# Attention with two head mixes and two MoE layers on one core: the second mix moved to a step's end, score and v pairs spread one a step, loads and early weights reordered

## The chip, the cores and the metric

One core of a Trainium2 chip runs the whole program. The metric is device time in microseconds (us) of one execution; the time of a kernel is the median of its runs. Engines are named as in the profile: PE is TensorE (matmuls), PEld its weight loads, DVE is VectorE, ACT is ScalarE, POOL is GpSimd, SP is SyncE, whose queue issues nearly all DMAs.

## What is computed

Attention over 2 batches, 12 heads, 448 rows and a head size of 64, with the scores mixed across heads before the softmax and the probabilities mixed across heads after it; then two feed-forward layers on the 896 x 768 result. The weights of these layers come as float64.

```python
scores = scale * np.matmul(q, k.transpose(0, 1, 3, 2))
scores = np.einsum('bhij,hg->bgij', scores, w_pre)      # first mix
scores = scores - np.max(scores, axis=-1, keepdims=True)
attn = np.exp(scores)
attn = attn / (np.sum(attn, axis=-1, keepdims=True) + 1e-09)
attn = np.einsum('bhij,hg->bgij', attn, w_post)         # second mix
out = np.matmul(attn, v)
...
h = x @ w_in                                            # 768 -> 2048
g = np.where(h > 0.0, h, np.exp(np.minimum(h, 0.0)) - 1.0)   # layer 1; layer 2: g = h * sigmoid(h)
x = g @ w_out                                           # 2048 -> 768
```

## The kernel before, in words

All order is written by hand: each engine runs its instructions in the order in which the program issues them.

**Attention in steps.** The 448 rows of a batch are cut into four tiles of 120, 120, 120 and 88 rows, eight tiles T = 0 to 7 in all. A tile's scores (12 heads x 448) are made by six "score pairs" (`qk_pair(T, p)`, L159: two heads each), scaled and copied to an SBUF tile `s` by ACT (head e = 0) and DVE (head e = 1) in `qk_evac` (L177). The mixes work on blocks of 10 rows x 12 heads; two blocks make a step. There are NB = 46 steps; the last step of each batch (22 and 45) has one block. The tiles begin at steps 0, 6, 12, 18, 23, 29, 35 and 41. For step s, `relayout(s)` (L196) brings two blocks of `s` by DMA on SP's queue into one of three buffers `blk`; it is issued two steps ahead. Then:

- `premix(s)` (L211): the first mix on PE into the two PSUM tiles `pre`; both are used by every step.
- `rmax(s)` (L218) on DVE: the negative maximum `nmx`; `exps(s)` (L224) on ACT: exponentials `pe` and their sums; `recip(s)` (L234): sum + 1e-9 and reciprocal on DVE, then two small scalings `krn` of the second mix's matrix on POOL (L243).
- `postmix(s)` (L246): the second mix on PE, 64 small matmuls on `pe` and `krn`, issued one step later, into one PSUM tile `post` of two banks; `post_evac` (L262) copies half of both banks to the tile `a` on ACT (L121), then the other half on DVE (L123).
- `av_pair(T, p)` (L274): the product with v for two heads of a finished tile.

One step of the loop issues, in this order: `premix(s)`, `postmix(s-1)`, the step's score pairs, v pairs and transposes (PE); `rmax(s)`, `exps(s)`, both halves of `post_evac(s-1)`, `qk_evac`, `recip(s)`, the v and transpose copies, `relayout(s+2)`, the step's loads. Tables `QK_AT`, `X_AT`, `KT_AT`, `D_AT` and `M_AT` say which step gets which pair, transpose, load or piece of weight work. Score pairs of tile T + 1 begin two steps ahead of tile T, and v pairs of tile T one step after tile T + 1 has begun, with what doesn't fit put into the last step; so step 21 has two score pairs and steps 23 and 46 two v pairs.

**Loads.** At the start q of tile 0, all of k of batch 0 (half of its DMAs issued from ACT's queue), the mix matrices; q has one buffer, so q of tile 1 is loaded when tile 0 is transposed. After the first two relayouts come v of batch 0 in two DMAs of 672 KB, then q of tile 2, which is transposed in steps 1 and 2.

**MoE.** Weights come as 64-bit words in chunks, 63 of them; a chunk is scaled on ACT (L480), turned into bits on DVE (L492, L494), and split into a high part (ACT, L508) and a low part (DVE, L514). A product is 18 matmuls (`moe_in`, L549): high x high, high x low, low x high over six slices. The first three chunks ("early", NE = 3) are loaded from step 39 on into the place of `s`, and one of their six products (chunk 1, first half of the rows) runs in thirds in the last steps. The input of the second half of the rows, `x1`, is split after the last step (`x1_hi`, `x1_lo`, L418).

## Time and profile before

| | us |
|---|---|
| runs | 728.5, 725.24, 725.59 |
| median | 725.59 |
| the profiled execution, its own time | 727.41 |
| its span, first to last instruction | 725.7 |
| PE busy in the span | 676.4 (93%) |
| DVE, ACT, POOL busy | 381.6, 343.7, 57.7 |

The span has two parts. From about 254 us to the end PE works through the MoE products without a pause. Before that lies the attention, where PE waits now and then. How the rows below are read: a row of the timeline gives start, length, engine, line, operation, out<-in and in brackets how long the engine sat idle before it and what ended that; a row of the waits gives who waited for whom, us in total, times, and the longest; a row of the chain is a piece of the path that ended last.

### The profile page before, as it was taken

How to read it: one execution, taken by the hardware profiler on the slowest of the kernel's cores; microseconds unless marked ns; L12 is line 12 of the kernel's file. 1: busy time of each engine (PE TensorE's matmuls, PEld its weight loads, DVE VectorE, ACT ScalarE, POOL GpSimd, SP SyncE). 2: the span in 40 equal slices, each digit the busy share in tenths (PEclk: the TensorE clock that was granted, in tenths of full speed). 3: DMA queues.
4: the chain of work that ended last, by engine and by line, in shares of the span. 5: the costliest groups of instructions: out<-in, count | busy, mean ns of one | idle time of the engine just before them, and what ended most of it. 6: DMA issues, size and time to landing. Idle time of an engine off the chain costs nothing.

```text
span 725.7 us, 16439 instructions
## 1 busy us (share of the span) xinstructions
PE 676.4 (93%) x6902; PEld 560.2 (77%) x6902; DVE 381.6 (53%) x771; ACT 343.7 (47%) x708; POOL 57.7 (8%) x118
## 2 busy tenths in 40 slices
PE   7667898788887899999999999999999999999998
PEld 3234555444554799999999999999999999999997
DVE  3535555555656556666664343336666667324500
ACT  2445666465675567666663233335555555313301
POOL 4011111122242100000000000000000000000000
PEclk8989999999999999999999999999999999999999
DMA  7545447424235133333353333333424345424202
GB/s 117 131 115 169 112 145 175 121 66 147 98 124 167 59 118 97 100 109 109 91 151 105 95 96 93 99 121 109 127 92 124 94 122 164 151 66 154 98 0 77
DMA packets 81866, 81.77 MB, mean 113 GB/s; under 512 B 25552, under 2 KB 77696, under 8 KB 81792
## 3 DMA queue, kind: packets, MB, share of 16 engines
q1 hardware_dynamic: 79008, 80.03, 37.0%
q10 hardware_dynamic: 2784, 0.69, 0.7%
q8 instruction: 54, 0.88, 0.5%
q14 instruction: 20, 0.16, 0.1%
HBM read 58.60 MB, written 2.75 MB: 85 GB/s over the span
## 4 chain that ended last, share of the span: by engine, by line
PE 78%; DVE 6%; ACT 6%; DMA 5%; issue 2%; POOL 2%; SPq 1%; ACTq 0%; POOLq 0%; DVEq 0%
PE ph L571 30%; PE po L624 16%; PE py L646 5%; PE py L644 5%; PE py L645 5%; ACT pe L230 3%; PE pre L216 3%; PE av L283 3%; PE pq L174 3%; PE post L256 3%; DMA blk<-s 3%; DVE a L123 2%; DVE s L183 2%; DMA qr<-in_q_dram 2%; DVE nmx L222 2%
## 5 line engine op out<-in xcount | busy, mean ns | idle before, releaser
L571 PE MATMUL ph<-x,we 128*128 128x448 f32 x1080 | 221.4, 367 | 0.0
L571 PEld LDWEIGHTS ph<-x,we 128*128 128x128 f32 x1080 | 202.8, 188 | 18.1
L624 PE MATMUL po<-g,we 128*128 128x448 f32 x468 | 101.3, 366 | 0.0
L256 PEld LDWEIGHTS post<-krn,pe 60*56 60x56 f32 (+1 forms) x2880 | 49.6, 134 | 59.7 <-POOL krn L243 57.5
L624 PEld LDWEIGHTS po<-g,we 128*128 128x128 f32 x468 | 87.9, 188 | 7.6
L230 ACT ACTIVATE pe<-pre,nmx 124x448 f32<-124x448 f32 (+1 forms) x92 | 57.5, 629 | 66.2 <-DVE nmx L222 54.6
L480 ACT ACTIVATE wr<-wr 128x384 f32<-128x384 f32 x126 | 67.3, 545 | 28.8 <-DMA wr<-in_moe_w_out_dram 24.9
L514 DVE TENSOR_TENSOR we<-wc,we 128x768 fp32r<-128x768 f32 (+1 forms) x63 | 58.7, 932 | 42.3 <-ACT we L508 39.4
L256 PE MATMUL post<-krn,pe 60*56 60x60 f32 (+1 forms) x2880 | 55.9, 222 | 26.6 <-POOL krn L243 26.2
L494 DVE SCALAR_TENSOR_TENSOR wc<-wr,wc 128x384 int32<-128x384 int32 x126 | 68.6, 545 | 5.3
L508 ACT CAST we<-wc 128x768 fp32r<-128x768 f32 (+1 forms) x63 | 50.8, 807 | 39.5 <-PE py L646 29.5
L123 DVE COPY a<-post 120x480 f32<-120x480 f32 (+1 forms) x46 | 30.9, 673 | 68.5 <-ACT a L121 68.5
L222 DVE TENSOR_REDUCE nmx<-pre 124x1 f32<-124x448 f32 (+1 forms) x92 | 53.0, 617 | 26.5 <-PE pre L216 25.9
L645 PE MATMUL py<-we,g 128*128 128x384 f32 x182 | 61.5, 338 | 0.0
L646 PE MATMUL py<-we,g 128*128 128x384 f32 x182 | 61.5, 338 | 0.0
L644 PE MATMUL py<-we,g 128*128 128x384 f32 x182 | 61.5, 338 | 0.0
L283 PEld LDWEIGHTS av<-a,v 120*64 120x64 f32 x768 | 37.6, 138 | 25.0 <-issue 17.3
L216 PE MATMUL pre<-blk,kpre 64*64 64x448 f32 (+1 forms) x360 | 51.2, 571 | 5.6 <-DMA blk<-s 4.6
L243 POOL TENSOR_SCALAR krn<-kps,sum 124x60 f32<-124x60 f32 (+1 forms) x92 | 41.1, 461 | 182.3 <-DVE sum L239 175.6
L174 PE MATMUL pq<-kt,qt 64*64 64x448 f32 (+2 forms) x384 | 50.1, 563 | 3.0 <-DVE s L183 2.3
L283 PE MATMUL av<-a,v 120*64 120x120 f32 (+1 forms) x768 | 46.8, 267 | 1.3 <-issue 1.3
L492 DVE TENSOR_SCALAR wc<-wr 128x384 int32<-128x384 int32 x126 | 43.7, 347 | 0.0
(86 smaller groups left out, 679.6 us busy)
## 6 DMA issues: line engine op xcount, KB each, us to landing
wr<-in_moe_w_in_dram SPq DMA_DIRECT2D x58, 384.0 KB
wr<-in_moe_w_out_dram SPq DMA_DIRECT2D x56, 384.0 KB
blk<-s SPq DMA_DIRECT2D x90, 210.0 KB
wr<-in_moe_w_out_dram SPq DMA_DIRECT2D x12, 256.0 KB
v<-in_v_dram SPq DMA_DIRECT2D x4, 672.0 KB
out_dram<-y SPq DMA_DIRECT2D x14, 192.0 KB
early<-in_moe_w_in_dram SPq DMA_DIRECT2D x6, 384.0 KB
qr<-in_q_dram SPq DMA_DIRECT2D x6, 360.0 KB
```

Source lines behind the costliest of these rows:

```text
L174: nc.tensor.matmul(pq[e][HS * c:HS * c + n], qT[T][half, p, HS * c:HS * c + n], kT[b, p][half], start=True, stop=True, tile_position=(e * ...
L216: nc.tensor.matmul(pre[s][r][HS * c:HS * c + HS], kpre[o], blkb[o, s % NBUF, c], start=True, stop=True, tile_position=(HS * r, HS * c))
L222: nc.vector.tensor_reduce(nmx[s][:n, r:r + 1], pre[s][r][:n], axis=AX.X, op=ALU.max, negate=True)
L230: nc.scalar.activation(t[:n], pre[s][r][:n], AF.Exp, bias=nmx[s][:n, r:r + 1], scale=1.0, accum_out=sums[s][:n, r:r + 1])
L256: nc.tensor.matmul(w[HS * u:HS * u + n, c, r * 240 + j * BW:r * 240 + (j + 1) * BW], pexp[s][r][o, j0:j0 + n], kr[s][r][o].rearrange("p h ...
L283: nc.tensor.matmul(avt[T][e * D:(e + 1) * D, p % 3, :m], vall[b][:NV, h, j], amap[T][:NV, j * H + h, :m], start=j == 0, stop=j == 3, tile_ ...
L494: nc.vector.scalar_tensor_tensor(cc, r[:, :, 1], 3, cc, op0=ALU.logical_shift_left, op1=ALU.bitwise_or)
L571: nc.tensor.matmul(ph, wt[:, kk * P:(kk + 1) * P], xq[hf, kk][:, xi], start=(n_ == 0), stop=(n_ + 1 == len(terms)))
L624: nc.tensor.matmul(po, wt[:, kk * P:(kk + 1) * P], g_out1(k0 + kk, gi, hf), start=(k0 == 0 and n_ == 0), stop=(k0 + kn == KF and n_ == 3 * ...
L644: nc.tensor.matmul(py, gh, hi[:, w_], start=(kf == 0), stop=False)
L645: nc.tensor.matmul(py, gh, lo[:, w_], start=False, stop=False)
L646: nc.tensor.matmul(py, gl, hi[:, w_], start=False, stop=(kf == KF - 1))
```

## The change

- A step now issues `premix(s)`, the score pair, the v pair, the transposes, any early MoE product, and `postmix(s-1)` as PE's last work; `post_evac(s-1)` is the last work of the step on ACT and DVE, behind the early weight work.
- `post` is two tiles of one bank, one for each block; ACT copies the first block and DVE the second. The score pair's two banks are separate tiles, too.
- One score pair and one v pair a step: score pairs run on without a gap (steps 0 to 39), v pairs from step 7 to 42, and those of tile 6 two a step in steps 43 to 45.
- q has two buffers; q of tile 1 is loaded right after the mix matrices, q of tile 2 right after the first two relayouts; v is loaded in four DMAs of 336 KB in steps 1 to 4 (batch 0) and 23 to 26 (batch 1).
- An exponential of one element on ACT stands ahead of ACT's loads; the clearing of `blk` goes from DVE to POOL.
- Early weights are loaded and turned in halves in steps 28 to 43, into the buffers of q and k. `x1` lies where `s` of the even tiles was, and its first 240 columns are split in steps 39 to 44 on ACT and POOL. Two of the early products (chunks 0 and 1, first half) run in thirds in steps 41 to 46.

```diff
-    cm_b, bp = pool("attn1", bufs=1, side="right")
+    cm_s0, sp0 = pool("s0", bufs=1, side="right")
+    cm_s1, sp1 = pool("s1", bufs=1, side="right")
...
-        r = raws["q", T] = bp.tile([TI, H, D], F32, name=f"qr{T}", tag="qr", bufs=1)
+        r = raws["q", T] = ap_.tile([P, H, D], F32, name=f"qr{T}", tag="qr", bufs=2)[:TI]
...
-        w = pst[s] = ps.tile([P, 2, 512], F32, name=f"post{s}", tag="post", bufs=1)
+        w = pst[s] = [ps.tile([P, 2, 4 * BW], F32, name=f"post{s}_{c}", tag=f"post{c}", bufs=1) for c in range(steps[s][2])]
...
-    def post_evac(s, r):
+    def post_evac(s):
...
-        o = amap[T][:NV, :, n * BI:(n + nc_) * BI].rearrange("p x (c r i) -> p c r x i", r=2, i=5)[:, :, r]
-        evac((nc.scalar, nc.vector)[r], o, pst[s][:NV, :nc_, r * 240:r * 240 + 240].rearrange("p c (x i) -> p c x i", i=5))
+        for c, w in enumerate(pst.pop(s)):
+            o = amap[T][:NV, :, (n + c) * BI:(n + c + 1) * BI].rearrange("p x (r i) -> p r x i", r=2)
+            evac((nc.scalar, nc.vector)[c], o, w[:NV].rearrange("p r (x i) -> p r x i", i=5))
...
+    wz = cp.tile([P, S], F16, name="wz")
+    nc.vector.memset(wz, 0.0)
+    nc.scalar.activation(kpre[0:1, 0:1], wz[0:1, 0:1], AF.Exp)
     load_q(0)
...
     load_mix()
+    load_q(1)
+    nc.gpsimd.memset(blkb[0:4], 0.0)
...
     for s in range(2):
         relayout(s)
-    for u in range(2):
-        load_v(0, u)
+    load_q(2)
...
-    load_q(2)
...
-                at(QK_AT, f - 2 + p, lambda T=T, p=p: qk_pair(T + 1, p))
...
+            if nqk >= 0:
+                at(QK_AT, nqk, lambda T=T, p=p: qk_pair(T + 1, p))
+            nqk += 1
...
+        for g in range(2):
+            at(D_AT, 1 + 2 * g + u, lambda u=u, g=g: load_v(0, u, g))
+            at(D_AT, first[4] + 2 * g + u, lambda u=u, g=g: load_v(1, u, g))
...
     def step(s):
         if s < NB:
             premix(s)
-        if 0 <= s - 1 < NB:
-            postmix(s - 1)
         run(QK_AT, s)
         run(X_AT, s)
         run(KT_AT, s)
+        run(F_AT, s)
+        if 0 <= s - 1 < NB:
+            postmix(s - 1)
         if s < NB:
             rmax(s)
             exps(s)
-        if 0 <= s - 1 < NB:
-            post_evac(s - 1, 0)
-            post_evac(s - 1, 1)
         qk_evac(0)
         qk_evac(1)
...
         relayout(s + 2)
         run(D_AT, s)
+        run(M_AT, s)
+        if 0 <= s - 1 < NB:
+            post_evac(s - 1)
...
+    for i, L in enumerate((-7, -4, -3, 0, 1, 4)):
+        n, j = divmod(i, 2)
+        at(M_AT, s6 + L + 2, lambda n=n, j=j: scale_w(n, j))
+        at(M_AT, s6 + L + 3, lambda n=n, j=j: bits_w(n, j))
+        at(M_AT, s6 + L + 3, lambda n=n, j=j: split_hi(n, j))
+        at(M_AT, s6 + L + 4, lambda n=n, j=j: split_lo(n, j))
+    for i, L in enumerate((-7, -4, -3, 0, 1, 4)):
+        at(M_AT, s6 + L, lambda i=i: load_w(i // 2, i % 2))
+    for n in range(2):
+        for part in range(3):
+            at(F_AT, NB - 5 + 3 * n + part, lambda n=n, part=part: moe_in(n, 0, n, 0, part))
```

PE's order around step 8, before: the end of the second mix of step 7, the step's score pair `pq`, v pair `av` and transpose `ptq`, and the first mix `pre` of step 9. The second mix of step 8 follows right behind it.

```order
L256 MATMUL post_795<-krn_1_784,pe_1_773 64x60 x2
L256 MATMUL post_795<-krn_1_784,pe_1_773 56x60 x2
L174 MATMUL pq_4_828<-kt_4_206,qt_356 64x448 x2
L174 MATMUL pq_4_828<-kt_4_206,qt_356 56x448 x2
L283 MATMUL av_0_752<-a_365,v_80 64x120 x8
L143 MATMUL ptq_1_841<-ident,qr_512 128x90 x3
L216 MATMUL pre_0_869<-blk,kpre 64x448
L216 MATMUL pre_1_870<-blk,kpre 64x448
```

The same step now: the first mix of step 8 (`pre_0_816`, `pre_1_817`), the same pairs and transpose, and only then the second mix of step 7.

```order
L214 MATMUL pre_0_816<-blk,kpre 64x448
L214 MATMUL pre_1_817<-blk,kpre 64x448
L172 MATMUL pq_4_0_822<-kt_4_212,qt_333 64x448
L172 MATMUL pq_4_1_823<-kt_4_212,qt_333 64x448
L172 MATMUL pq_4_0_822<-kt_4_212,qt_333 56x448
L172 MATMUL pq_4_1_823<-kt_4_212,qt_333 56x448
L280 MATMUL av_0_745<-a_388,v_83 64x120 x8
L145 MATMUL ptq_1_836<-ident,qr_527 128x90 x3
L254 MATMUL post_0_840<-krn_0_806,pe_0_798 64x60
L254 MATMUL post_1_841<-krn_0_806,pe_0_798 64x60
```

Between a step's first mix and its second mix on PE there stood one step's pairs; now there are two steps' pairs.

DVE's order in step 8, before: maximum, copy `a` of the second mix, copy `s` of the scores, then the two operations on `sum` that POOL's `krn` waits for.

```order
L222 TENSOR_REDUCE nmx_845<-pre_0_789 124x1
L222 TENSOR_REDUCE nmx_845<-pre_1_790 124x1
L123 COPY a_775<-post_795 120x2x48x5
L183 TENSOR_SCALAR s_554<-pq_4_828 120x448
L238 TENSOR_SCALAR sum_848<-sum_848 124x2
L239 RECIPROCAL sum_848<-sum_848 124x2
```

DVE in step 8 now:

```order
L220 TENSOR_REDUCE nmx_874<-pre_0_816 124x1
L220 TENSOR_REDUCE nmx_874<-pre_1_817 124x1
L181 TENSOR_SCALAR s_539<-pq_4_1_823 120x448
L236 TENSOR_SCALAR sum_877<-sum_877 124x2
L237 RECIPROCAL sum_877<-sum_877 124x2
L125 COPY a_813<-post_1_841 120x2x48x5
```

The copy of the second mix went from ahead of the reciprocal to the end of the step, ahead of the next step's maximum.

SP's queue behind the first two relayouts, before: both v loads, then q of tile 2, then the relayouts of steps 2 to 5.

```order
L204 DMA blk<-s_137 120x1x448 x4
L96 DMA v_80<-in_v_dram 56x12x256 x2
L81 DMA qr_262<-in_q_dram 120x12x64
L204 DMA blk<-s_137 120x1x448 x8
L81 DMA qr_512<-in_q_dram 88x12x64
```

SP's queue from q of tile 2 on, now:

```order
L82 DMA qr_249<-in_q_dram 120x12x64
L202 DMA blk<-s_167 120x1x448 x4
L98 DMA v_83<-in_v_dram 56x6x256
L202 DMA blk<-s_167 120x1x448 x2
L98 DMA v_83<-in_v_dram 56x6x256
L202 DMA blk<-s_167 120x1x448 x2
L82 DMA qr_527<-in_q_dram 88x12x64
```

q of tile 2 went ahead of v; the first two of v's four pieces stand between relayouts here, and the other two follow q of tile 3 (`qr_527`) in the same way.

## Rows read from the trace of the kernel before

**Rows 1.** Windows: stretch, its length, busy us (instructions) of PE, PEld, DVE, ACT, POOL, clock.

```profile
25.97:61.86 35.89, 23.92 (x503) 11.97 (x503) 16.36 (x38) 15.59 (x40) 5.75 (x13) 0.90 0.62 159
61.86:213.77 151.91, 131.98 (x3205) 76.64 (x3203) 85.75 (x199) 92.50 (x233) 32.91 (x73) 1.00 0.40 121
213.77:254.10 40.33, 32.08 (x705) 23.79 (x703) 23.04 (x52) 21.72 (x49) 10.75 (x16) 0.96 0.41 126
254.10:725.70 471.60, 468.09 (x2384) 439.33 (x2382) 246.11 (x466) 205.93 (x374) 0.00 (x0) 1.00 0.35 106
```

**Rows 2.** Timeline, PE in steps 8 and 9 (one step without, one with a stall).

```profile
68.31 0.98 PE L216 MATMUL pre<-blk,kpre 64*64 64x448 f32 x8
...
69.27 1.09 PE L256 MATMUL post<-krn,pe 60*64 60x60 f32 x62
...
70.18 0.56 PE L174 MATMUL pq<-kt,qt 64*56 64x448 f32 x2
...
71.10 1.04 PE L283 MATMUL av<-a,v 120*64 120x120 f32 x16
...
72.08 0.45 PE L143 MATMUL ptq<-ident,qr 90*128 90x90 f32 x3
...
72.46 0.98 PE L216 MATMUL pre<-blk,kpre 64*64 64x448 f32 x8
...
74.18 1.09 PE L256 MATMUL post<-krn,pe 60*64 60x60 f32 x62 [0.74 <-POOL krn L243]
...
76.98 0.98 PE L216 MATMUL pre<-blk,kpre 64*64 64x448 f32 x8
```

**Rows 3.** Timeline, the other engines between the first mix at 68.31 and its `krn`.

```profile
69.40 1.16 DVE L222 TENSOR_REDUCE nmx<-pre 124x1 f32<-124x448 f32 x2 [0.81 <-PE pre L216]
...
70.77 0.62 ACT L230 ACTIVATE pe<-pre,nmx 124x448 f32<-124x448 f32 x1
...
72.04 0.68 DVE L123 COPY a<-post 120x480 f32<-120x480 f32 x1 [1.48 <-ACT a L121]
...
73.69 0.83 POOL L243 TENSOR_SCALAR krn<-kps,sum 124x60 f32<-124x60 f32 x2 [4.07 <-DVE sum L239]
```

**Rows 4.** Waits in 61.86 to 213.77: who for whom, us in all, times, longest.

```profile
DVE a L123 <- ACT a L121: 49.2, 33, 1.7
...
PE post L256 <- POOL krn L243: 16.1, 23, 1.7
...
PE pq L174 <- DVE s L183: 2.3, 1, 2.3
...
PE av L283 <- issue: 1.3, 1, 1.3
```

**Rows 5.** Chain that ended last, 20 to 62: start, length, what.

```profile
23.02 2.81 DMA blk<-s
...
27.82 11.30 DMA qr<-in_q_dram
...
53.13 5.28 DMA blk<-s
```

**Rows 6.** Timeline, PE: the first mix of step 6.

```profile
58.55 1.76 PE L216 MATMUL pre<-blk,kpre 64*64 64x448 f32 x8 [0.95 <-DMA blk<-s]
```

**Rows 7.** Windows of 10 us, the one behind the wait for q.

```profile
40.00:50.00 10.00, 9.03 (x172) 4.90 (x171) 4.31 (x10) 5.62 (x14) 0.83 (x2) 0.78 0.37 133
```

**Rows 8.** Chain, 210 to 256: a relayout behind the early weights.

```profile
216.04 7.89 DMA blk<-s
```

**Rows 9.** Timeline, PE: a third of an early product; v pairs of the last tile.

```profile
239.10 1.49 PE L571 MATMUL ph_qk<-x,we 128*128 128x448 f32 x6
...
250.31 3.86 PE L283 MATMUL av<-a,v 120*64 120x88 f32 x96
```

**Rows 10.** The page's groups: MoE products; weight bits of half a chunk.

```profile
L571 PE MATMUL ph<-x,we 128*128 128x448 f32 x1080 | 221.4, 367 | 0.0
...
L494 DVE SCALAR_TENSOR_TENSOR wc<-wr,wc 128x384 int32<-128x384 int32 x126 | 68.6, 545 | 5.3
```

**Rows 11.** Timeline, ACT at the start.

```profile
7.86 1.28 ACT L121 ACT_TABLE_LOAD   x1 [7.86 <-DMA k<-in_k_dram]
```

More of the change, by code (lines that the diff above doesn't have):

```diff
@@ L58, in attn_moe_moe @@
     vall = [ap_.tile([P, H, 4, D], F32, name=f"v{b}") for b in range(B)]
-    blkb = bp.tile([P, NBUF, 2, S], F32, name="blk")
+    blkb = ap_.tile([P, NBUF, 2, S], F32, name="blk")
     tiles = [(b, t) for b in range(B) for t in range(4)]
@@ L163, in qk_pair @@
         if T not in smap:
[L164 to L169 removed]
+            smap[T] = (sp0, sp1)[T % 2].tile([P, H, S], F32, name=f"s{T}", tag="s")
+        pq = [ps.tile([P, S], F32, name=f"pq{T}_{p}_{e}", tag="pre" if where == "pre" else f"{where}{e}", bufs=2 if where == "pre" else 1) for e in range(2)]
         for c in range(2):
@@ L291, in av_evac @@
             c = slice(t * TI, t * TI + m)
-            if T + 1 == len(tiles):
+            if T + 2 >= len(tiles):
                 x = x1_tile()
@@ L351, in at @@
         d.setdefault(int(step), []).append(f)
-    for T in range(NT_):
+    nqk, nav = -2, 0
+    for T in range(NT_ - 1):
         b, t = tiles[T]
         f, l = first[T], last[T]
-        if T + 1 < NT_:
-            for p in range(NP):
-                if T == 0 and p < 2:
-                    continue
-                at(QK_AT, f - 2 + p, lambda T=T, p=p: qk_pair(T + 1, p))
-            for p in range(NP):
-                at(X_AT, first[T + 1] + 1 + min(p, last[T + 1] - first[T + 1]), lambda T=T, p=p: av_pair(T, p))
+        for p in range(NP):
+            if nqk >= 0:
+                at(QK_AT, nqk, lambda T=T, p=p: qk_pair(T + 1, p))
+            nqk += 1
+        for p in range(NP):
+            nav = max(nav + 1, first[T + 1] + 1)
+            if T + 2 == NT_:
+                at(X_AT, NB + (-3, -3, -2, -2, -1, -1)[p], lambda T=T, p=p: av_pair(T, p, ("av", "tr")[p // 3]))
+            else:
+                at(X_AT, nav, lambda T=T, p=p: av_pair(T, p))
         if T + 2 < NT_:
@@ L480, in scale_w, with w_bits @@
         nc.scalar.activation(hf, hf, AF.Prelu, scale=2.0 ** -112, alpha=2.0 ** 32)
-    def bits_w(n, part=None, ops=(0, 1)):
-        tl = rawt[n]
-        tot = sum(x[2] for x in tl)
-        if n not in wbits:
-            wbits[n] = w_tile(n, 0, "wc").bitcast(F32), tot
-        c = wbits[n][0].bitcast(I32)
-        for r, o, m in tl if part is None else tl[part:part + 1]:
-            cc = c[:, o:o + m]
+    wbits = {}
+    def w_bits(n, part):
+        if n < NE:
+            if (n, part) not in wbits:
+                wbits[n, part] = ap_.tile([P, 4 * P], I32, name=f"wc{n}_{part}", tag="kr", bufs=2)
+            return wbits[n, part]
+        if n not in wbits:
+            wbits[n] = mo["ws"].tile([P, KC * P], I32, name=f"wc{n}", tag="wc", bufs=2)
+        return wbits[n][:, part * 384:]
+    def bits_w(n, part=None, ops=(0, 1)):
+        for j, (r, o, m) in enumerate(rawt[n]):
+            if part not in (None, j):
+                continue
+            cc = w_bits(n, j)[:, :m]
             if 0 in ops:
```

182 lines of the change are left out of this document (76 added, 106 removed).

## The prediction, made before the changed kernel was run

> **What bounds the kernel now.** I first cut the span into stages by PE's work, with a table of windows [rows 1]. From 254.10 us on PE is busy 468.09 of 471.60 us: only fewer matmuls shorten that part. Before it PE is idle 12.0 of 35.89 us in steps 0 to 6, 19.9 of 151.91 in steps 7 to 39, and 8.3 of 40.33 in the rest of the attention. The change works there, and 40 us is nearly all there is to win without taking work off PE.
>
> Then the timeline of two steps [rows 2]. Step 8 lasts from 68.31 to 72.46, 4.15 us, without a pause: first mix .96 (69.27 - 68.31), second mix .91, score pair .92, v pair .98, transpose .38 (start to start, so that overlap is counted once). Without the transpose that is 3.77 us, the length at which PE is full. Step 9 is 4.52 long, .74 of it idle in the middle of its second mix, waiting for POOL's `krn`. The waits [rows 4] show 23 such stops, 16.1 us in all. The timeline of the other engines tells why [rows 3]: from the first mix at 68.31 the maximum starts at 69.40, the second exponential ends at 71.39 (70.77 + .62), DVE then stands 1.48 behind ACT's half of the copy `a`, and only behind its own half come the sums and, at 73.69 + .83 = 74.52, the last `krn`. That is 6.2 us behind the first mix, while PE wants it one step and a first mix later, at about 4.15 + .96 = 5.1. DVE's stop behind ACT comes in 33 steps, 49.2 us in all [rows 4].
>
> Third, the chain of waits from 20 to 62 us [rows 5]: q of tile 2 takes 11.30 us from issue to landing behind both v loads, and a later relayout 5.28 instead of the 2.81 of the first. A table of 10 us windows [rows 7] adds that the granted clock was .78 from 40 to 50, behind that wait, so that PE was busy 9.03 of 10 us with less work in it. The first mix of step 6 [rows 6] still waits for a relayout.
>
> **The change part by part.**
>
> *Steps 7 to 39.* The second mix moves behind the pairs, so `krn` is wanted 3.77 us into the next step or later: 3.77 + 2.86 = 6.6 us behind the first mix in a full step (2.86 is 3.77 less the mix itself). And it comes earlier: the copy `a`, with its 1.48 of waiting and .68 of copying [rows 3], is no longer ahead of the sums, so 6.2 becomes about 4.1 to 5.5 (the score copy may still stand ahead). The wait for `krn` goes with over 1 us to spare. What is late next? A step's first mix writes the PSUM tiles that the exponentials of the step before read. That ring is 3.08 (68.31 to 71.39), and was 3.31 from step 6 to step 7 (58.55 to 61.86) [rows 1, 6]: below 3.77, so PE covers it by .46. A copy of the second mix now stands right ahead of the next maximum on DVE, and delays it only if PE's last matmuls end late against the next first mix; PE has .96 of first mix to cover the .68. So the steps should be full: 33 x 3.77 = 124.4, less .9 for the single-block steps, and 16 transposes (k's of batch 1 and q's) x .38 = 6.1, together 129.6. As a cross-check, PE's busy time there is 131.98, and it loses one v pair (.98) to the later stage. On top I put three costs that no row prices: the first relayouts of tiles 4 to 7 now follow the last score pair of their tile at once (0 if they land like the first at 2.81, up to 4 x 2.5 = 10 if like the one at 5.28 [rows 5]; taken 1.0); the weight work in ACT's and DVE's steps (six halves x three DVE operations x .55 [rows 10] = 9.8 if it all fell into the ring, 0 if it fits; taken 1.0, since DVE is busy just 85.75 of 151.91 us [rows 1]); and stops without a cause such as the 1.3 in a v pair [rows 4], kept at 1.3. The stop of 2.3 behind two score pairs goes. That makes 132.9 against 151.91: **-19.0**.
>
> *Steps 0 to 6.* q of tile 1 and 2 come ahead of v, and v comes in four pieces between relayouts, so the 11.30 goes. There are no v pairs here, so a step is shorter than the ring, and the ring sets it: 7 x 3.31 = 23.2. What is left of the loads: 1704 KB (360 of q, 2 x 672 of v) took 11.30, so a piece of 336 KB is 2.2 us and q of tile 3 (264 KB) 1.7; a relayout behind both could be that much later, and the clearing of q's spare rows stands behind `krn` on POOL. From 0 to 5.3 (3 us above 2.81 at one place, 2.3 of it again at another); taken 2. 25.2 against 35.89: **-10.7**. With the idle stop gone the clock of .78 should not come back, either; this sits in the sum already, since the steps are priced by the ring.
>
> A rule speaks against the four pieces. The Trainium skill (DMA: Bandwidth & Descriptors, "Anatomy of one DMA") gives each DMA a fixed cost of some 2.0 us, and its "Bandwidth" section asks for 1 MiB or more. If two more DMAs cost that on the path, an estimate from the page would be 2 x 2.0 = 4 more, 689. No row here shows that cost by itself.
>
> *From step 40 to the end of the last v pairs.* No score pairs are left: 3.4 (step 40, the ring) + 2 x 4.15 (2.85 of mixes and v pair and a third of a product, six matmuls of 221.4 / 1080 = .205 [rows 10] = 1.23, or 1.3 against the row's 1.49 with its end [rows 9]) + 2 x 5.13 (two v pairs and a third) + 4.65 (the single block) + 1.75 (the last second mix and third) + .7 for the last copy + 3.8 (v pairs of the last tile, [rows 9]) + .5 = 33.4 against 40.33: **-6.9**. The 7.89 of a relayout behind the early weights [rows 8] goes, since these are loaded from step 28 on, in halves.
>
> *MoE.* The first half of chunk 0's product has moved into the steps: 18 x .205 = 3.7: **-3.7**. The rest of x1's split is shorter at the end; its cover is the products of the first half of the rows.
>
> *Prologue.* The exponential table, loaded at 7.86 for 1.28 behind ACT's DMA issues [rows 11], now comes ahead of them, but delays them by as much: -1.3 to +1.3; taken **-.4**.
>
> Sum: -.4 - 10.7 - 19.0 - 6.9 - 3.7 = -40.7, and 727.41 - 40.7 = 686.7. The profiled execution is 1.8 above the median of the runs, so the forecast is **685**.
>
> **The rivals.**
>
> *The ring isn't covered.* If the copy of the second mix stands fully ahead of the maximum, the ring is 3.08 + .68 = 3.76, as long as a full step, and nothing is to spare: all 9.8 of the weight work and 7 x (3.76 - 3.31) = 3.2 in steps 0 to 6 come on top: 685 + 13 = 698. For it speaks DVE's new order; against it that PE's first mix runs in the time of the copy.
>
> *Late relayouts.* The first relayouts of the tiles take 5.28 instead of 2.81: 4 x 2.5 = +10, 695. For it: the loads in SP's queue stand right around them; against it: most relayouts in steps 7 to 39 made nobody wait [rows 4].
>
> *Small gain.* `krn` still ends late, since POOL has got the clearing and the x1 split: if the 16.1 of [rows 4] and half of the gain in steps 0 to 6 stay, 685 + 16 + 5 = 706; 703 to 722.
>
> *Slower.* Every relayout lands late. It reads `s`, writes a buffer that the first mix of three steps before has read, and is wanted by its own: three steps must hold one first mix and one landing, so at 3.77 a landing may take 3 x 3.77 - .96 = 10.3. If the added pieces in the queue made landings 13.8 like those of the q behind v (11.30 [rows 5]) and worse, a step would be 4.92, and 40 steps x 1.15 = +46: 731. It decides from 10.3 on; the only landings near it are 11.30 behind 1.3 MB, and 7.89 [rows 5, 8], and no piece is that large now. No change at all would need 40.7 / 40 = 1.02 more a step, landings of 13.4.
>
> *PE isn't full.* In steps 7 to 39 PE's weight loads are busy 76.64 of 151.91 us, half, where matmuls show 131.98 [rows 1]. If matmuls only look long and could close up, the ring would set the step: 33 x 3.31 + 6.1 = 115, some 18 less than my 132.9, so 667. Against it: the steps without a stop last 4.15 with their pieces back to back [rows 2]. The Trainium skill (Perfetto Trace Analysis, "Identifying the Most-Contended Engine") holds by this rule that matmul busy time is a poor measure of what TensorE has left, and names the weight loads' busy share instead.
>
> **How the numbers follow.** Chances: forecast .63, its own range 678 to 692 (relayouts, loads and weight work each from 0 to half their bounds, prologue both ways); ring not covered .18; late relayouts .08; small gain .05; slower .04; PE not full .01; no change .01. The range of 678 to 700 takes in the first three. What a measurement of this kernel can tell from no change is about 0.5%, 3.6 us: faster .95, within .01, slower .04.
>
> **What would show it.** Right: windows of steps 7 to 39 at about 133 us with hardly a wait of PE for `krn`; full steps of 3.77 with no pause; steps 0 to 6 at 3.3 to 3.6 each, their chain through maximum and exponentials, and clock at 1.00; no landing above 6 us ahead of 60 us; the end of the attention near 214. Wrong: PE's first mixes waiting for exponentials all through (ring), or for `blk` in the first steps of a tile (relayouts); the second mix waiting for `krn` at step ends (small gain); a MoE part that isn't 3.7 shorter, or that now starts with a wait for weights; steps below 3.7.

## The result, and the profile after

The changed kernel takes 691.56 us (median of 690.68 to 692.18) where the kernel before took 726.68 beside it: ratio 0.9515, 95% interval 0.9487 to 0.9542. The forecast was 685, with a range of 678 to 700. Three single executions lie far off the others of their kernel and are left out of the ratios here and below: 769.08 and 944.78 of the kernel before, and 3170.97 of `a4_clear_early`. The profiled execution has a span of 689.9 against 725.7, and the windows of its stages (columns as in [rows 1]) stand against that group one by one:

```profile
23.09:52.91 29.82, 24.41 (x498) 13.26 (x502) 17.16 (x40) 15.78 (x42) 5.75 (x13) 0.91 0.72 200
52.91:185.99 133.08, 129.03 (x3200) 83.67 (x3195) 91.88 (x206) 92.93 (x236) 34.32 (x73) 0.98 0.50 148
185.99:222.24 36.25, 34.48 (x751) 25.76 (x741) 18.23 (x43) 19.54 (x51) 12.98 (x22) 1.00 0.34 111
222.24:689.90 467.66, 464.31 (x2365) 435.91 (x2364) 245.57 (x465) 205.56 (x374) 0.00 (x0) 1.00 0.35 106
```

| stage | before | now | change | forecast |
|---|---|---|---|---|
| prologue, to the first mix of step 0 | 25.97 | 23.09 | -2.9 | -.4 |
| steps 0 to 6 | 35.89 | 29.82 | -6.1 | -10.7 |
| steps 7 to 39 | 151.91 | 133.08 | -18.8 | -19.0 |
| step 40 to the last v pairs | 40.33 | 36.25 | -4.1 | -6.9 |
| MoE | 471.60 | 467.66 | -3.9 | -3.7 |
| span | 725.7 | 689.9 | -35.8 | -40.7 |

What PE waited for in the whole execution (us in all, times, longest), against [rows 4]: the wait for `krn`, 26.2 us in 33 stops in the whole execution before, is gone altogether, and relayouts are what is left.

```profile
PE pre L214 <- DMA blk<-s: 8.6, 5, 3.7
PE post L254 <- ACT a L123: 1.3, 2, 1.0
```

PE in step 9, against [rows 2]: the first mix of step 9 starts at 61.60, that of step 10 at 65.16, with no pause. A full step is 3.56, not 3.77.

```profile
61.60 0.56 PE L214 MATMUL pre<-blk,kpre 64*64 64x448 f32 x2
...
62.37 0.98 PE L172 MATMUL pq<-kt,qt 64*56 64x448 f32 x8
63.27 1.04 PE L280 MATMUL av<-a,v 120*64 120x120 f32 x16
64.25 1.09 PE L254 MATMUL post<-krn,pe 60*64 60x60 f32 x62
65.16 0.56 PE L214 MATMUL pre<-blk,kpre 64*64 64x448 f32 x2
```

Behind the first relayout, three stand as long pieces in the chain that ended last (start, length). They answer to [rows 5]: the 11.30 of q is gone, but the relayout of step 6 now takes 7.44.

```profile
41.04 7.44 DMA blk<-s
...
113.83 4.16 DMA blk<-s
...
137.90 5.46 DMA blk<-s
```

The reason for the first is in the timelines of POOL and of SP's queue:

```profile
37.04 0.84 POOL L241 TENSOR_SCALAR krn<-kps,sum 124x60 f32<-124x60 f32 x2 [2.41 <-DVE sum L237]
37.94 0.73 POOL L81 MEMSET qr<- 26x768 f32 x1
```

```profile
31.09 1.67 SPq L202 DMA_DIRECT2D blk<-s  x2
38.69 0.30 SPq L82 DMA_DIRECT2D qr<-in_q_dram  x1
39.05 0.99 SPq L98 DMA_DIRECT2D v<-in_v_dram  x1
40.15 1.68 SPq L202 DMA_DIRECT2D blk<-s  x2
```

The load of q of tile 3 waits until POOL has cleared its spare rows (37.94 + .73 = 38.67), which stands behind `krn` of step 3. Until 38.69 nothing gets past it on SP's queue, and then 264 KB of q and 336 KB of v go ahead of the relayout of step 6. PE waits twice, and runs at half its clock for a while behind that; the window's row has the granted clock, .58, as its third number from the end:

```profile
46.60 0.97 PE L214 MATMUL pre<-blk,kpre 64*64 64x448 f32 x4 [3.74 <-DMA blk<-s]
48.53 1.01 PE L214 MATMUL pre<-blk,kpre 64*64 64x448 f32 x2 [0.96 <-DMA blk<-s]
```

```profile
46.60:52.91 6.31, 5.35 (x76) 2.76 (x80) 2.12 (x5) 1.77 (x5) 0.00 (x0) 0.58 0.66 218
```

### The profile page after: what moved, and what is told of

The parts are those of the page before. It is cut to its first block, busy times and chain, and to the rows that moved or that the text cites. A ratio compares the mean times of both kernels' runs of the same rounds, so it can differ in the third digit from the quotient of the medians.

```text
span 689.9 us, 16546 instructions
## 1 busy us (share of the span) xinstructions
PE 671.3 (97%) x6902; PEld 566.5 (82%) x6902; DVE 381.1 (55%) x771; ACT 342.0 (50%) x716; POOL 63.6 (9%) x125
## 4 chain that ended last, share of the span: by engine, by line
PE 91%; DMA 4%; ACT 2%; DVE 1%; issue 1%; POOL 0%; ACTq 0%; DVEq 0%; POOLq 0%
PE ph L578 34%; PE po L631 17%; PE py L653 6%; PE py L651 6%; PE py L652 6%; PE pre L214 6%; PE post L254 6%; PE av L280 5%; PE pq L172 4%; DMA blk<-s 3%; ACT pe L228 1%; PE ptk L134 1%; PE ptq L145 1%; DMA k<-in_k_dram 1%; DVE nmx L220 0%
## 5 line engine op out<-in xcount | busy, mean ns | idle before, releaser
L578 PE MATMUL ph<-x,we 128*128 128x448 f32 x1152 | 237.7, 367 | 0.0
L578 PEld LDWEIGHTS ph<-x,we 128*128 128x128 f32 x1152 | 215.8, 188 | 20.1 <-issue 0.8
L483 ACT ACTIVATE wr<-wr 128x384 f32<-128x384 f32 x132 | 70.5, 546 | 29.8 <-DMA wr<-in_moe_w_out_dram 25.6
L505 DVE SCALAR_TENSOR_TENSOR wc<-wr,wc 128x384 int32<-128x384 int32 x132 | 72.2, 547 | 5.5
L214 PE MATMUL pre<-blk,kpre 64*64 64x448 f32 (+1 forms) x360 | 55.5, 568 | 9.3 <-DMA blk<-s 8.6
L172 PE MATMUL pq<-kt,qt 64*64 64x448 f32 (+2 forms) x384 | 55.6, 566 | 0.2 <-ACT qt L123 0.2
L503 DVE TENSOR_SCALAR wc<-wr 128x384 int32<-128x384 int32 x132 | 45.8, 347 | 0.0
L593 ACT ACTIVATE e<-ph 128x448 f32<-128x448 f32 x32 | 17.4, 545 | 50.6 <-PE ph L578 50.6
```

The source lines that it names most:

```text
L172: nc.tensor.matmul(pq[e][HS * c:HS * c + n], qT[T][half, p, HS * c:HS * c + n], kT[b, p][half], start=True, stop=True, tile_position=(e * ...
L214: nc.tensor.matmul(pre[s][r][HS * c:HS * c + HS], kpre[o], blkb[o, s % NBUF, c], start=True, stop=True, tile_position=(HS * r, HS * c))
L483: nc.scalar.activation(hf, hf, AF.Prelu, scale=2.0 ** -112, alpha=2.0 ** 32)
L505: nc.vector.scalar_tensor_tensor(cc, r[:, :, 1], 3, cc, op0=ALU.logical_shift_left, op1=ALU.bitwise_or)
L578: nc.tensor.matmul(ph, wt[:, kk * P:(kk + 1) * P], xq[hf, kk][:, xi], start=(n_ == 0), stop=(n_ + 1 == len(terms)))
```

## The experiments

Two questions were open. Which edit took the wait for `krn` away, and why is the stage of steps 7 to 39 as short as forecast although its steps aren't? And where do the 6.6 us between forecast and result lie? All ratios are against the kernel before, run beside each. The table at the end of this section has the stages of all kernels.

**Old place of the second mix.** `a1_old_order`:

```diff
             premix(s)
+        if 0 <= s - 1 < NB:
+            postmix(s - 1)
         run(QK_AT, s)
...
-        if 0 <= s - 1 < NB:
-            postmix(s - 1)
         if s < NB:
             rmax(s)
             exps(s)
+        if 0 <= s - 1 < NB:
+            post_evac(s - 1)
...
-        if 0 <= s - 1 < NB:
-            post_evac(s - 1)
```

> The changed kernel with the second mix back right behind the first mix and its copies back behind the exponentials; separate banks, pairs, loads and early weights stay as changed. Theory (the place of the second mix took away the wait for krn): the 16.1 us of that wait come back, and the full step is 3.77 again instead of 3.56, another 33 x .21 = 7: about 708 to 715. Rival (with separate banks krn is in time anyway, since DVE no longer waits 1.48 for ACT's copy): only the 7 of the longer step: 698, with less than 3 us of PE waiting for krn.

694.06, ratio 0.9577 (0.9523 to 0.9632), an interval that overlaps the changed kernel's. The rival is right in kind, since the 16 us of waits don't come back, but not in size: full steps are 3.56 to 3.59 here too, so its 7 us aren't there, and PE waits 6.0 us for `krn` in the whole execution, where it said less than 3. PE's waits in steps 7 to 39 (`issue`: the profile names no cause):

```profile
PE pre L214 <- DMA blk<-s: 4.5, 2, 3.5
PE post L254 <- POOL krn L241: 4.0, 4, 1.4
PE post L254 <- issue: 1.6, 1, 1.6
```

Four stops for `krn`, in steps 7, 25, 31 and 37, one or two steps behind the first step of a tile (6, 23, 29, 35); why there is open. In steps 8 to 24 there is none.

**One tile for the second mix.** `b3_one_tile`:

```diff
-        w = pst[s] = [ps.tile([P, 2, 4 * BW], F32, name=f"post{s}_{c}", tag=f"post{c}", bufs=1) for c in range(steps[s][2])]
+        w = pst[s] = ps.tile([P, 2, 512], F32, name=f"post{s}", tag="post", bufs=1)
...
-        for c, w in enumerate(pst.pop(s)):
...
+        w = pst.pop(s)
+        for r in range(2):
```

The order stays as changed, and so do the separate tiles of the score pairs.

> The changed kernel with the second mix in one tile of two banks again, half of both banks copied by ACT and then the other half by DVE; the order stays as changed. Theory (the new order needs the separate banks): DVE's copy waits for ACT's, now right ahead of the next maximum, so the ring is 3.08 + 1.2 or more and sets a step of 4.2 to 4.5 instead of 3.56: 712 to 725. Rival (PE's first mix covers that too): 691 to 694.

703.01, ratio 0.9693 (0.9652 to 0.9734): between the two. PE doesn't wait for `krn` once, as in the changed kernel. Until step 18 most steps are as short as in the changed kernel, as the rival says. Most of the cost lies in steps 32 to 40, with steps of up to 5.6: there DVE's copy waits for ACT's, PE's second mix for DVE's, and the exponentials for the maximum behind that copy.

```profile
172.07 0.69 DVE L125 COPY a<-post 120x480 f32<-120x480 f32 x1 [1.56 <-ACT a L123]
...
172.91 1.15 PE L258 MATMUL post<-krn,pe 60*64 60x60 f32 x64 [1.03 <-DVE a L125]
...
173.38 0.64 ACT L232 ACTIVATE pe<-pre,nmx 124x448 f32<-124x448 f32 x1 [1.34 <-DVE nmx L224]
```

**Both.** `c1_old_order_one_tile`, the two edits above together.

> The changed kernel with both the old place of the second mix and its copies (as a1_old_order) and the one tile of two banks (as b3_one_tile). Each alone cost 2 to 4 and 11 to 12 us. Theory (either the new place or the separate tiles is enough to have krn in time, and only without both does the wait come back): the 16.1 us of waits for krn come back on top, 710 to 720, with 20 or more stops for krn. Rival (the costs simply add): 704 to 707.

717.21, ratio 0.9895 (0.9858 to 0.9932). The wait for `krn` is back, as the theory says: 26.9 us in 26 stops in the whole execution, 20.6 in 21 of them in steps 7 to 39. From 45 to 195 us, which the rows below cover, DVE stands behind ACT 31 times. In steps 7 to 39 the two edits cost 8.5 and 10.2 alone (141.6 and 143.2 against 133.1), and 25.6 together. So either one, the new order or separate tiles, is enough to have `krn` nearly always in time.

```profile
DVE a L125 <- ACT a L123: 49.8, 31, 3.0
...
PE post L258 <- POOL krn L245: 17.4, 18, 1.6
```

**The other way round: tiles alone, in the kernel before.** `c2_before_two_tiles` gives the second mix, and the few score pairs and products that use the same banks, its two tiles and changes nothing else:

```diff
-        w = pst[s] = ps.tile([P, 2, 512], F32, name=f"post{s}", tag="post", bufs=1)
+        w = pst[s] = [ps.tile([P, 2, 4 * BW], F32, name=f"post{s}_{c}", tag=f"post{c}", bufs=1) for c in range(steps[s][2])]
...
-        evac((nc.scalar, nc.vector)[r], o, pst[s][:NV, :nc_, r * 240:r * 240 + 240].rearrange("p c (x i) -> p c x i", i=5))
...
+            evac((nc.scalar, nc.vector)[r], o, pst[s][r][:NV].rearrange("p r (x i) -> p r x i", i=5))
```

> The kernel before with nothing changed but the second mix in two tiles of one bank, one for each block, ACT copying the first and DVE the second. Theory (the separate tiles free DVE of its 1.48 behind ACT, so sums and krn come 1.2 to 1.5 earlier and PE's wait of .74 in every second step goes, without any new order): 725 - 16 = 709, down to 705. Rival (the wait for krn needs the new order): 721 to 726.

721.81, ratio 0.9947 (0.9922 to 0.9971): here the rival is right on the number, but not for its reason. DVE no longer waits for ACT's copy `a`, yet now it waits for ACT's half of the score copy, 1.28 us ahead of the sums, and PE still for `krn`:

```profile
72.05 0.63 DVE L186 TENSOR_SCALAR s<-pq 120x448 f32<-120x448 f32 x1 [1.28 <-ACT s L184]
72.59 0.16 DVE L241 TENSOR_SCALAR sum<-sum 124x2 f32<-124x2 f32 x1
...
73.14 0.83 POOL L246 TENSOR_SCALAR krn<-kps,sum 124x60 f32<-124x60 f32 x2 [3.95 <-DVE sum L242]
...
73.62 1.09 PE L259 MATMUL post<-krn,pe 60*64 60x60 f32 x62 [0.62 <-POOL krn L246]
```

In the old tile of the second mix each half lay in both banks, so the edit also gives each engine a bank of its own. The halves of a score pair lay in two banks already, and DVE's copy waited all the same. So `d1_before_all_tiles` splits the tile of the score pair as well:

```diff
-            w = ps.tile([P, 2, 512], F32, name=f"pq{T}_{p}", tag=where, bufs=1)
-            pq = [w[:, e, :S] for e in range(2)]
+            pq = [ps.tile([P, S], F32, name=f"pq{T}_{p}_{e}", tag=f"{where}{e}", bufs=1) for e in range(2)]
```

> The kernel before with separate tiles of one bank for the second mix (as c2_before_two_tiles) and for the two halves of a score pair as well; order, pairs and loads stay as before. In c2 DVE no longer waited 1.48 for ACT's copy a, but then .6 to 1.3 for ACT's half of the score copy, and krn came no earlier. Theory (both shared tiles hold the sums back, one behind the other; without either krn is in time, at the old order): PE's 16 us of waits for krn go, 722 - 12 to 15 = 707 to 710. Rival (the order or the spread of pairs is what matters): 718 to 722.

702.25, ratio 0.9691 (0.965 to 0.9732), below what the theory asked for. Steps 7 to 39 take 130.79, less than in the changed kernel. In its step 10 `krn` starts right behind the sums' reciprocal, which ends at 71.30 (the row names ACT's copy `a`, which ends at 71.33), and ends at 71.49 + .83 = 72.32; the second mix, which starts at 71.99, isn't stopped by it any more. That `krn` ends 4.7 behind the first mix of its own step (67.64). It is 4.7 in most steps of d1, a1 and the changed kernel, and 6.2 in the kernel before. The waits of the stage hold no line of PE for `krn`.

```profile
70.94 0.16 DVE L237 TENSOR_SCALAR sum<-sum 124x2 f32<-124x2 f32 x1
...
71.49 0.83 POOL L242 TENSOR_SCALAR krn<-kps,sum 124x60 f32<-124x60 f32 x2 [3.10 <-ACT a L121]
71.99 1.12 PE L255 MATMUL post<-krn,pe 60*64 60x60 f32 x59
```

```profile
58.80:189.59 130.79, 127.69 (x3204) 78.51 (x3203) 85.29 (x199) 89.28 (x231) 32.98 (x73) 1.00 0.47 139
```

This settles the first question: two thirds of the whole gain (23 of 35 us) are reached with tiles alone, with order, pairs and loads of before. Either shared tile is enough to hold the sums back at the old order (c2 and c1). The new order takes the wait away by itself as well (b3), but then the shared tile costs some 12 us elsewhere. What the new order would do with the score pair's tile shared, too, wasn't run; and for the second mix no run tells the tile from the bank.

**Which pair comes first.** `a3_v_first` asks why a step is 3.56:

```diff
-        run(QK_AT, s)
         run(X_AT, s)
+        run(QK_AT, s)
```

> The changed kernel with a step's v pair ahead of its score pair on PE; all else as changed. Theory (a full step is 3.56 instead of 3.77 because the first mix and the score pair, both of 64 x 448, now follow each other and one change of the kind of matmul is saved): a full step is 3.75 again, 33 x .2 = 6.6 more: 698. Rival (the shorter step comes from the banks or from the second mix being last): 3.56 stays, 691 to 692.

695.33, ratio 0.9582 (0.9543 to 0.9622). The time is nearer to the theory, but its mechanism falls: steps without a transpose are 3.56 here as well. Most of the 16 steps with one are .15 longer (4.24 against 4.09, or 4.16 against 4.02); .11 of this is the score pair, which takes .79 (66.00 - 65.21) ahead of a second mix and .90 ahead of a transpose. Another 2.4 lie in steps 28 and 29, where PE waits for a relayout: 13.6 for the two against 11.1.

```profile
65.21 0.97 PE L172 MATMUL pq<-kt,qt 64*64 64x448 f32 x8
66.00 1.04 PE L254 MATMUL post<-krn,pe 60*56 60x60 f32 x62
...
68.77 0.97 PE L172 MATMUL pq<-kt,qt 64*64 64x448 f32 x8
69.67 0.60 PE L134 MATMUL ptk<-ident,kr 112*128 112x112 f32 x4
```

So 3.56 isn't a matter of order, and where the .21 went is told by step 8 in two other kernels of the same PE order. In d1 it lasts 3.94 with its transpose (63.70 to 67.64), in the kernel before 4.15. The first mix takes .96 in the kernel before [rows 2] and .80 in d1:

```profile
63.70 0.98 PE L215 MATMUL pre<-blk,kpre 64*64 64x448 f32 x8
64.50 1.04 PE L255 MATMUL post<-krn,pe 60*64 60x60 f32 x62
...
67.64 0.61 PE L215 MATMUL pre<-blk,kpre 64*64 64x448 f32 x4
```

And in the kernel before, POOL's first of two `krn` ends near 69.20 (68.78 and half of .84), right where the second mix starts (69.27):

```profile
68.78 0.84 POOL L243 TENSOR_SCALAR krn<-kps,sum 124x60 f32<-124x60 f32 x2 [3.20 <-DVE sum L239]
```

The step that I took for one without a stop had one of .16, which PE's idle time doesn't show, since the end of the first mix lies .98 behind its start and so covers it; the other .05 lie in the second mix (.91 against .86). Another row of the same trace did show it, that of PE's weight loads, and the waits count them in all 33 steps of the stage, where PE was idle for `krn` in 23 (16.1 us):

```profile
69.27 1.00 PEld L256 LDWEIGHTS post<-krn,pe 60*64 60x64 f32 x63 [0.75 <-POOL krn L243]
```

```profile
PEld post L256 <- POOL krn L243: 40.1, 33, 2.5
```

Not all of these 40.1 us cost time. In d1 the weight loads wait for `krn` in 31 steps (13.4 us), up to .58 in full steps of 3.55 to 3.59. An estimate from that: what lies above .58 adds up to 21.6 in the kernel before and to .9 in d1, and the stage is 21.1 shorter in d1. In the changed kernel and in b3 they don't wait for `krn` at all in this stage.

**Clearing q's spare rows earlier.** `a4_clear_early`:

```diff
+                if T % 4 == 0:
+                    at(D_AT, f + 1, lambda T=T: clear_q(T + 3))
                 at(D_AT, f + 3, lambda T=T: load_q(T + 3))
```

`clear_q` is the clearing that stood in `load_q`.

> The changed kernel with the spare rows of q of tiles 3 and 7 cleared on POOL two steps earlier; the loads keep their places in SP's queue. Theory (the load of q, and with it SP's whole queue, waits for POOL's clearing behind krn, and the relayouts of steps 6 and 28 behind it): the waits of 3.74 and .96 ahead of steps 6 and of 2.32 in step 28 go, and the clock of .58 behind the first: 680 to 684. Rival (the bytes of q and v ahead of the relayout make it late, not the clearing): the loads only go earlier and 689 to 692 stays.

683.98, ratio 0.9417 (0.9341 to 0.9493); the median of the three executions that the ratio uses is 682.33. That is the theory's size, and half of its places. Steps 28 and 29 have no wait any more; ahead of step 6 and in it there are still 2.42 and .46, and a relayout still takes 7.49 with no queue behind POOL. So both were right: the clearing, and the bytes.

```profile
37.19 7.49 DMA blk<-s
```

**Loads later, or earlier.** `c3_loads_later`, on top of a4, puts q behind the first relayout of a tile, and the second halves of v two steps later in batch 0 and three in batch 1 (not four, as its text says):

```diff
-                at(D_AT, f + 3, lambda T=T: load_q(T + 3))
+                at(D_AT, f + 4, lambda T=T: load_q(T + 3))
...
-            at(D_AT, 1 + 2 * g + u, lambda u=u, g=g: load_v(0, u, g))
-            at(D_AT, first[4] + 2 * g + u, lambda u=u, g=g: load_v(1, u, g))
+            at(D_AT, 1 + 4 * g + u, lambda u=u, g=g: load_v(0, u, g))
+            at(D_AT, first[4] + 5 * g + u, lambda u=u, g=g: load_v(1, u, g))
```

> The kernel of a4_clear_early with the loads of q one step later, behind the first relayout of a tile, and v's second halves four steps later. Theory (what was left of the waits for relayouts, 2.42 and .46 ahead of steps 6 and 7 and .6 ahead of step 23, and the low clock behind them, comes from the bytes of q and v in the queue): 684 - 4 to 8 = 676 to 680, first mixes of steps 6 and 23 without a wait. Rival (what is left is the relayout's own 2.8 us): 682 to 685.

686.38, ratio 0.9471 (0.9432 to 0.9509). Steps 0 to 6 are 2.0 shorter than in a4 and step 23 is free of its wait, but steps 7 to 39 are 4.0 longer: steps 29 to 31, where early weights are loaded beside v's second halves, take 3.2 more, and step 8 stops for 1.39 for a cause that the profile doesn't name (as step 6 for 2.08). `d2_loads_early`, on top of a4, goes the other way:

```diff
+    for g in range(2):
+        for u in range(2):
+            load_v(0, u, g)
...
+    load_q(2)
     for s in range(2):
         relayout(s)
-    load_q(2)
...
-                at(D_AT, f + 3, lambda T=T: load_q(T + 3))
+                at(D_AT, f + (1 if T == 3 else 3), lambda T=T: load_q(T + 3))
...
-            at(D_AT, 1 + 2 * g + u, lambda u=u, g=g: load_v(0, u, g))
-            at(D_AT, first[4] + 2 * g + u, lambda u=u, g=g: load_v(1, u, g))
+            at(D_AT, (13, 14, 17, 18)[2 * g + u], lambda u=u, g=g: load_v(1, u, g))
```

> The kernel of a4_clear_early with v of batch 0 and q of tile 2 loaded ahead of the first relayout, where the DMA engines moved nothing (16 to 20 us), v of batch 1 in steps 13 to 18 instead of 23 to 26, and q of tile 6 in step 19 instead of 21. Theory (in steps 1 to 6 and 22 to 29 the relayouts are late because 5.3 MB must go through in some 26 us; bytes moved out of these stretches end the waits, and with them the low clock): steps 0 to 6 in 23 instead of 27.4 and steps 22 to 26 some 2 shorter: 676 to 679. Rival (a relayout takes that long by itself, or v now makes the first relayout late): 682 to 687.

686.09, ratio 0.9473 (0.9437 to 0.9509). Steps 0 to 6 take 23.06, as the theory says (and as the ring of 3.31 gives, 23.2). But all of it is paid ahead, as the rival says of the first relayout: the first mix of step 0 starts at 27.21. The windows show the DMA engines full from 14 to 24 us (share 1.03 to 1.07, 178 to 210 GB/s), of which the changed kernel leaves 16 to 20 nearly free (share .00 and .03), and the first relayout behind that takes 6.96. First the changed kernel, then d2 twice:

```profile
16.00:18.00 2.00, 2.00 (x20) 0.79 (x20) 1.18 (x3) 1.31 (x3) 0.00 (x0) 1.00 0.00 0
```

```profile
16.00:18.00 2.00, 2.00 (x22) 0.79 (x20) 1.18 (x3) 1.25 (x3) 0.00 (x0) 1.00 1.03 206
...
20.00:22.00 2.00, 1.76 (x17) 0.48 (x16) 1.17 (x3) 0.83 (x2) 0.00 (x0) 1.00 1.06 199
```

So `f1_half_v_early`, again on top of a4, moves half of v, and the second half into steps 1 and 2:

```diff
+    for u in range(2):
+        load_v(0, u, 0)
...
+    load_q(2)
     for s in range(2):
         relayout(s)
-    load_q(2)
...
-                at(D_AT, f + 3, lambda T=T: load_q(T + 3))
+                at(D_AT, f + (4 if T == 3 else 3), lambda T=T: load_q(T + 3))
...
-            at(D_AT, 1 + 2 * g + u, lambda u=u, g=g: load_v(0, u, g))
+            if g:
+                at(D_AT, 1 + u, lambda u=u, g=g: load_v(0, u, g))
```

> The kernel of a4_clear_early with only the first halves of v of batch 0 (2 x 336 KB) and q of tile 2 loaded ahead of the first relayout, the second halves in steps 1 and 2, and q of tile 6 in step 22, behind the first relayout of its tile. In d2 all of v and q of tile 2 (1704 KB) went ahead: the waits of steps 5 and 6 were gone, and the first relayout landed 4.2 later. Theory (only the bytes count: from 16 to 20 us some 0.2 MB a us can go for nothing, so about 1 MB is free and what is over pushes the first relayout): first mix of step 0 at 21 to 22, steps 0 to 6 in 23 to 24, 677 to 680. Rival (waits only move, whatever is ahead): 683 to 687.

681.16, ratio 0.9374 (0.9354 to 0.9393), the shortest of all and 10 us below the changed kernel; its interval lies below those of c3 and d2, but inside that of a4. Neither text has it whole: steps 0 to 6 are 23.34 without a wait, but the first mix of step 0 starts at 24.35 instead of 21 to 22, since the first relayout still takes 5.89. One megabyte ahead, of d2's 1.7, was still too much. Steps 7 to 39 are at 127.49.

```profile
24.35:47.69 23.34, 23.33 (x502) 13.29 (x503) 16.45 (x38) 14.82 (x40) 5.77 (x13) 0.89 0.56 175
47.69:175.18 127.49, 126.84 (x3187) 81.99 (x3187) 92.15 (x209) 94.01 (x239) 34.45 (x73) 1.00 0.52 157
```

**Steps 40 and 41.** In the changed kernel they take 4.11 and 5.46. PE waits 1.02 for ACT's copy there, and the next first mix is stretched over 2.23:

```profile
189.15 1.15 PE L254 MATMUL post<-krn,pe 60*64 60x60 f32 x64 [1.02 <-ACT a L123]
190.10 2.23 PE L214 MATMUL pre<-blk,kpre 64*64 64x448 f32 x8
```

`c4_copy_first` and, on top of d2, `d3_early_split_later` tried to shorten this:

```diff
-        run(M_AT, s)
         if 0 <= s - 1 < NB:
             post_evac(s - 1)
+        run(M_AT, s)
```

> The changed kernel with the copies of the second mix ahead of the step's early weight work on ACT and DVE, instead of behind it. Theory (in steps 35 to 41 ACT's copy comes late behind weight work, PE's second mix waits 1.0 for it and the ring is lengthened): 2 to 3 less than the changed kernel, 688 to 690, steps 35 to 41 at 3.6 to 4.2. Rival (ACT and DVE then stand idle until the second mix ends and the weight work gets into the next step's exponentials): the same steps 0.3 to 0.5 longer, 693 to 696.

```diff
-        at(M_AT, s6 + 4 + p, lambda p=p: x1_conv(p))
+        at(M_AT, s6 + 6 + p, lambda p=p: x1_conv(p))
```

> The kernel of d2_loads_early with the split of the second half's input (a copy on ACT, a subtraction on POOL) in steps 41 to 46 instead of 39 to 44. Theory (steps 36 to 41 are long by 3 us since ACT has more to do than a step holds, so its copy of the second mix and the next exponentials come late): steps 40 and 41, 9.6 in the changed kernel, lose .8 to 1.5, and d2 is undercut by that: 675 to 678. Rival (it is the weights' work alone, or what moves is late at the end): as d2, or 1 us more.

690.45 (ratio 0.9526, 0.9493 to 0.9558), no difference from the changed kernel that its interval allows to tell, and 686.18 (0.9469, 0.9435 to 0.9503), that of d2. In c4 the wait for the copy is gone and one of .69 for the exponentials stands in its place, with steps 40 and 41 at 4.31 and 5.65; in d3 the 1.02 is still there, and the two steps are 4.11 and 5.35. So it isn't the split of x1 that sets step 40; step 41 still holds its first piece in d3. Whether the weights' work on ACT or the split of the other half's input sets these steps wasn't tried.

Stages of all kernels in us, cut at the first mixes of steps 0, 7 and 40, and at the end of the last v pairs. Each row is one execution, and executions of one kernel differ by .9 (d3) to 6.6 us (a1), so that a difference of a few us between two rows isn't shown by them alone. In MoE a1 and c1 are 2.2 shorter: the first 540 matmuls start .203 apart there and .207 in the changed kernel, and why is open.

| | prologue | 0 to 6 | 7 to 39 | to the last v | MoE |
|---|---|---|---|---|---|
| before | 25.97 | 35.89 | 151.91 | 40.33 | 471.60 |
| c2 second mix in two tiles | 25.68 | 35.87 | 151.32 | 37.08 | 471.61 |
| d1 score pair in two, too | 23.88 | 34.92 | 130.79 | 36.76 | 471.60 |
| changed | 23.09 | 29.82 | 133.08 | 36.2 | 467.7 |
| a1 old order | 21.68 | 30.74 | 141.57 | 34.40 | 465.56 |
| b3 one tile | 21.56 | 29.53 | 143.24 | 38.75 | 467.84 |
| c1 both | 21.65 | 31.18 | 158.68 | 37.56 | 465.55 |
| a3 v pair first | 21.51 | 29.21 | 139.32 | 36.18 | 467.71 |
| c4 copy ahead of weights | 21.24 | 29.71 | 132.93 | 36.57 | 467.71 |
| a4 clearing early | 21.13 | 27.44 | 128.13 | 36.20 | 467.71 |
| c3 loads later | 23.15 | 25.45 | 132.13 | 36.19 | 467.71 |
| d2 loads early | 27.21 | 23.06 | 129.01 | 36.10 | 467.72 |
| d3 x1 split later | 27.71 | 23.31 | 130.09 | 36.09 | 467.72 |
| f1 half of v early | 24.35 | 23.34 | 127.49 | 36.19 | 467.71 |

## Why the prediction was right, and where it was not

The direction, the size and the range held: 691.56 lies in 678 to 700, 6.6 above the forecast and just inside the likeliest case's own 678 to 692. The stages make up 4.9 of the 6.6. The other 1.7 come from what was taken off because the profiled execution before lay above its median; the changed kernel's lies on it (691.6). By its steps:

**Steps 7 to 39: right in sum (132.9 against 133.08), wrong in both parts.** The step that failed first is "that is 3.77 us, the length at which PE is full". I took step 8 for one without a stop, by its idle time of zero, and it holds a hidden wait for `krn` of .16. The full step is 3.56; a transpose adds .38 to .53, say .5, and the v pairs of tile 3, of 88 rows, make six steps .22 shorter (steps 26 and 27 take 3.34 in f1). With 33 x 3.56 - .9 + 16 x .5 - 6 x .22 = 123.3 the floor lies 6 below my 129.6. The second failure has the other sign: for stops I took 1.0 + 1.0 + 1.3 = 3.3, and 133.1 - 123.3 = 9.8 were there. Some 5.6 of them are relayouts late behind POOL's clearing and the loads of q (127.49 in f1; 128.13 in a4, which moves the clearing alone). That my terms came out at the right sum is chance.

**The wait for `krn`: gone, as forecast and in the way forecast, but the order earns little of the time.** I wrote that `krn` comes earlier, at 4.1 to 5.5 instead of 6.2, and is wanted later, at 6.6: in step 9 of the changed kernel the first mix starts at 61.60, `krn` ends 4.7 behind that, and the second mix starts 6.2 behind it. The new order alone does that without a stop (b3). But it isn't needed: undoing it costs only 8.5 us of the stage (a1), 4.5 of a1's waits there are for relayouts, and steps 8 to 24 have no stop for `krn`. Splitting two tiles in the old kernel takes the stops of the whole stage away (d1). The line of the diff on them, "the score pair's two banks are separate tiles, too", got no term in my sum at all; in the old order it is worth some 19 us on top of c2. It could have been read ahead of time: in the kernel before all 46 copies `a` on DVE and 46 of its 48 copies `s` wait for a semaphore of ACT, in the changed kernel all for one of PE. [Rows 3] showed the 1.48 of `a`; behind it the wait of `s` was hidden, since whoever waits first shows alone.

**Steps 0 to 6: mechanism right, size off.** "a relayout behind both could be that much later, and the clearing of q's spare rows stands behind `krn` on POOL", from 0 to 5.3, taken 2: it was 29.82 - 23.2 = 6.6, above my upper end. The place was the one named. The two effects added (the queue held until 38.69, then 600 KB ahead), and "the clock of .78 should not come back" failed: behind 4.7 us of waiting it was .58 for 6.3 us. With the bytes away the stage is at 23.06 and 23.34, so the ring's 23.2 was right, even with a low clock in the first steps there (4.02 and 3.98 in f1 against 3.31 and 3.71 in a4).

**Late relayouts were the rival that came true in part.** It was priced at +10 for the first relayouts of four tiles; over both stages they cost, with the low clock behind them, some 6.5 (29.82 - 23.34) + 5.6 = 12 us. That the result isn't 695 or more is the step of 3.56.

**The ring stayed covered**, as long as tiles are separate: with one tile (b3) the copy right ahead of the maximum does what that rival says, though only where early weights share the steps, 143.2 instead of 133.1.

**The end of the attention** was forecast 2.8 too short: steps 40 and 41 took .7 and 1.3 more than worked out (whether it is weight work at a bound that I took as covered isn't shown); the last step and the v pairs behind it took another .9.

**MoE:** -3.9 for -3.7; the term of 18 matmuls was right. **Prologue:** -2.9 for -.4, and most of it goes with the clock that each profiled execution was granted (no run varies that alone). In the first 21 us it was .84 in the kernel before and in c2, where step 0 starts at 25.97 and 25.68; .92 in the changed kernel, c3 and d1 (23.09, 23.15, 23.88); and 1.00 in the six others without early loads (21.13 to 21.68). The changed kernel, c3 and a4 have the same start, so the level isn't a matter of the kernel alone. At .92 the changed kernel is .8 ahead of d1, which starts as the kernel before does but for its tiles. The table's load made the first copy of q come 1.0 earlier.

**The rival of closing matmuls** gave 667 by steps at the ring, and that falls: with tiles of 120 rows no kernel has a full step below 3.54. The Trainium skill (Perfetto Trace Analysis, "Identifying the Most-Contended Engine") would have TensorE judged by its share of the peak and by the busy time of its weight loads. These are busy 83.67 of 133.08 us now, 63%, and 2.34 of 3.56, 66%, in the full step from 61.60 to 65.16, while no run got that step any shorter; here the length of a step without a stop was the better measure. The fixed cost of some 2.0 us for a DMA that the Trainium skill gives (DMA: Bandwidth & Descriptors, "Anatomy of one DMA", there for DMAs of the gpsimd path, where these are SP's) isn't isolated by any run; d2 and f1 load v in the same four pieces, and steps 0 to 6 have no wait for a relayout.

## What to carry to other kernels

When two engines copy the two halves of one PSUM tile, look at what the second one waits for; if it is the first engine and not PE, give each half a tile and a bank of its own before rearranging anything else. A wait can hide a second one of the same kind right behind it, so that splitting one tile alone shows next to nothing, and a step without idle time isn't yet a step without a wait: read the row of PE's weight loads, too, and compare the step with the same step elsewhere. Ahead of a load that goes into a queue shared with the critical transfers, ask what that load itself waits for, and move bytes to where the DMA engines rest, no more than fit there.
